# Reading all weights in rows next to each other per partition, and transposing 32x32 blocks on VectorE, in a fused decode layer

## The chip, the cores and the metric

The kernel runs on one core of a Trainium2 chip. The metric is the device time of one execution in microseconds (us), as a median over runs; nearly all executions of one kernel agree within 0.3%.

A profile is one execution on the chip with its records. Its span (138.0 us before) is about 2 us shorter than the timed run. Engines: PE (matmul), PEld (weight load, overlaps PE), DVE (VectorE), ACT (ScalarE), POOL (GpSimd); SPq is the queue of SyncE, from which the loads are issued.

## The reference, cut to what matters

```
h  = x  + attention(layernorm(x)) @ wo        x: 4 x 1 x 1024
h2 = h  + (silu(n @ w1) * (n @ w3)) @ w2      n = layernorm(h)

attention: 32 query heads, 4 KV heads of 128, batch 4, the last 2048 positions of the cache
wq 1024x4096   wo 4096x1024   w1, w3 1024x3584   w2 3584x1024   K, V 4x4x2048x128 each, all bf16
```

There are four rows of activations and 55.6 MB of weights and cache, each byte of which is used once.

## The kernel before

One pool of ten 16 KiB slots per partition takes all loads. They stand in one plan (wq, K, V, wo, w1, w3, w2) and are issued from one queue, ten at the start and then one whenever a slot has been used.

```python
wq_v = A_wq.rearrange("(p kc) n -> p kc n", kc=KC)            # 2 adjacent rows a load: 16 KiB runs
wo_v = A_wo.rearrange("(h4 p r) n -> p h4 r n", p=P, r=RPO)   # 4 adjacent rows:  8 KiB runs
w2_v = B_w2.rearrange("(j p i) n -> p j i n", p=P, i=IF)      # 7 adjacent rows: 14 KiB runs
# w1, w3: rows c*256 ... c*256+255 as "(p r) f -> p r f", r=2:  14 KiB runs, one contiguous block
# K: "g (pp j) d -> pp g (j d)": 16 KiB runs     V: "g (p j) d -> p g j d": 4 KiB runs
...
plan = (
    [("wq", load_wq, (c,)) for c in range(KC // KPC)]
    + [("k", load_k, (b,)) for b in range(B)]
    + [("v", load_v, (b,)) for b in range(B)]
    + [("wo", load_wo, (c,)) for c in range(Hq // HPC)]
    + [("w1", load_w13, (0, c)) for c in range(KC // KPC)]
    + [("w3", load_w13, (1, c)) for c in range(KC // KPC)]
    + [("w2", load_w2, (j, [IF] if j < JG - 1 else [4, 2, 1])) for j in range(JG)]
)
```

Which rows of a weight lie on which partition decides how the activation that is multiplied with it must lie. Before, that costs four selection matmuls and four copies for o, two PE transposes and a copy for the second layernorm, and seven PE transposes and a copy for the gate:

```python
for r in range(RPO):
    nc.tensor.matmul(o4_ps[:, r, :, :, :], lhsT=sel[:, r, :, :], rhs=OT_sb[:], start=True, stop=True)
for hh in range(RPO):
    nc.vector.tensor_copy(out=o4[hh * MP : (hh + 1) * MP, ...], in_=o4_ps[hh * MP : (hh + 1) * MP, :, :, hh, :])
...
for i in range(IF):
    nc.tensor.transpose(out=hg_ps[:, i, :], in_=hg_v[:, i, :], identity=ident[:])
nc.vector.tensor_copy(out=hgT[:, :, :, :, 0], in_=hg_ps[:]...)
```

Of the kernel before, what the change touches and what calls it, by code (L numbers as in the profile page):

```python
# [10 lines left out]
P = 128  # L11
# [8 lines left out]
def kernel(  # L20
# [47 lines left out]
    QD = P // JG  # L68
    CQ = Hq * Dh // JG
# [3 lines left out]
    IF = CF // P  # L73
    PK = P // Hkv
    JK = W // PK
    assert CQ == REP * Dh and CF == IF * P and HF <= 512


    KPC = 2
    HPC = 8  # L80
    RPO = 4
    assert CG == KPC * P
    wq_v = A_wq.rearrange("(p kc) n -> p kc n", kc=KC)
    wo_v = A_wo.rearrange("(h4 p r) n -> p h4 r n", p=P, r=RPO)
    w2_v = B_w2.rearrange("(j p i) n -> p j i n", p=P, i=IF)

    def load_wq(c):
        wq_t = stream.tile([P, KPC, Hq * Dh], BF16, tag="s")
        nc.sync.dma_start(out=wq_t[:], in_=wq_v[:, c * KPC : (c + 1) * KPC, :])
        return wq_t  # L90

    def load_k(b):

        k_t = stream.tile([P, JK * Dh], BF16, tag="s")
        nc.sync.dma_start(
            out=k_t[:],
            in_=A_k_cache[b, :, Sk - W : Sk, :].rearrange("g (pp j) d -> pp g (j d)", pp=PK),
        )
        return k_t

    def load_v(b):
        v_t = stream.tile([P, Hkv, NK, Dh], BF16, tag="s")
        nc.sync.dma_start(
            out=v_t[:],
            in_=A_v_cache[b, :, Sk - W : Sk, :].rearrange("g (p j) d -> p g j d", j=NK),
        )
        return v_t

    def load_wo(c):
        wo_t = stream.tile([P, HPC // RPO, RPO, D], BF16, tag="s")  # L110
        nc.sync.dma_start(
            out=wo_t[:], in_=wo_v[:, c * (HPC // RPO) : (c + 1) * (HPC // RPO), :, :]
        )
        return wo_t

    def load_w13(i, c):
        w13_t = stream.tile([P, KPC, F], BF16, tag="s")
        nc.sync.dma_start(
            out=w13_t[:],
            in_=(B_w1, B_w3)[i][c * KPC * P : (c + 1) * KPC * P, :].rearrange(  # L120
                "(p r) f -> p r f", r=KPC
            ),
        )
        return w13_t

    def load_w2(j, pieces):
        w2_t = stream.tile([P, IF, D], BF16, tag="s")
        i = 0
        for n in pieces:
            nc.sync.dma_start(out=w2_t[:, i : i + n, :], in_=w2_v[:, j, i : i + n, :])  # L130
            i += n
        return w2_t

    plan = (
        [("wq", load_wq, (c,)) for c in range(KC // KPC)]
        + [("k", load_k, (b,)) for b in range(B)]
        + [("v", load_v, (b,)) for b in range(B)]
        + [("wo", load_wo, (c,)) for c in range(Hq // HPC)]
        + [("w1", load_w13, (0, c)) for c in range(KC // KPC)]
        + [("w3", load_w13, (1, c)) for c in range(KC // KPC)]  # L140
        + [("w2", load_w2, (j, [IF] if j < JG - 1 else [4, 2, 1])) for j in range(JG)]
# [4 lines left out]
    def load_next(n=1):  # L146
        for _ in range(n):
            if cursor[0] < len(plan):
                kind, f, args = plan[cursor[0]]
                loaded.setdefault(kind, []).append(f(*args))  # L150
                cursor[0] += 1
# [12 lines left out]
    for j in range(JG):  # L164
        nc.scalar.dma_start(
            out=x_q[QD * j : QD * j + B, :], in_=x_flat[:, j * CG : (j + 1) * CG]
        )
# [20 lines left out]
    for kc in range(KC):  # L188
# [9 lines left out]
    nc.vector.memset(qz[:], 0.0)  # L198

    RS = QD // B  # L200
    spread = const.tile([P, JG, B, RS], FP32)
    nc.vector.memset(spread[:], 0.0)
    nc.vector.tensor_copy(
        out=spread[:, :, :, 0], in_=ident[:].rearrange("p (j x) -> p j x", j=JG)[:, :, :B]
    )
    hgT = act.tile([P, IF, JG, B, RS], BF16)
    nc.gpsimd.memset(hgT[:], 0.0)

    sel = const.tile([P, RPO, RPO, P // RPO], BF16)
    ident_r = ident[:].rearrange("p (m r) -> p r m", r=RPO)  # L210
    for hh in range(RPO):
        nc.vector.tensor_copy(out=sel[:, :, hh, :], in_=ident_r)
# [12 lines left out]
    for kc in range(KC):  # L225
        wq_t = loaded["wq"][kc // KPC]
        for hf in range(CQ // 512):
            for g in range(JG):
                c0 = g * CQ + hf * 512
                nc.tensor.matmul(  # L230
                    q_ps[QD * g : QD * g + B, hf * 512 : (hf + 1) * 512],
                    lhsT=xnT[:, kc, :],
                    rhs=wq_t[:, kc % KPC, c0 : c0 + 512],
                    start=(kc == 0),
                    stop=(kc == KC - 1),
                )
        if kc % KPC == KPC - 1:
            load_next()
# [33 lines left out]
    for u, (b, n) in enumerate(units):  # L272
        k_v = loaded["k"][b][:].rearrange("p (j d) -> p j d", d=Dh)
# [15 lines left out]
        if n == NSB - 1:  # L289
            load_next()  # L290
# [35 lines left out]
    for b in range(B):  # L326
# [10 lines left out]
        load_next()  # L337
    OT_sb = act.tile([P, Hq, B], BF16)
    nc.vector.tensor_copy(out=OT_sb[:].rearrange("p h b -> p b h"), in_=OT_ps[:])

    o4_ps = psA.tile([P, RPO, Hq // RPO, RPO, B], FP32, tag="kt3")
    for r in range(RPO):
        nc.tensor.matmul(o4_ps[:, r, :, :, :], lhsT=sel[:, r, :, :], rhs=OT_sb[:], start=True, stop=True)
    o4 = act.tile([P, Hq // RPO, RPO, B], BF16)
    MP = P // RPO
    for hh in range(RPO):
        nc.vector.tensor_copy(
            out=o4[hh * MP : (hh + 1) * MP, :, :, :].rearrange("p h r b -> p r h b"),
            in_=o4_ps[hh * MP : (hh + 1) * MP, :, :, hh, :],
        )  # L350
# [5 lines left out]
    nc.vector.memset(y_ps[:], 0.0)  # L356
    y2_ps = psB.tile([P, CG], FP32, tag="y2")
    g_ps = psB.tile([P, 2, 512], FP32, tag="g")
    nc.vector.memset(g_ps[:], 0.0)
    u_ps = psB.tile([P, 2, 512], FP32, tag="u")  # L360
    nc.vector.memset(u_ps[:], 0.0)
    for h4 in range(Hq // RPO):
        wo_t = loaded["wo"][h4 * RPO // HPC]
        for r in range(RPO):
            for j in range(JG):
                nc.tensor.matmul(  # L366
                    y_ps[QD * j : QD * j + B, :],
                    lhsT=o4[:, h4, r, :],
                    rhs=wo_t[:, h4 % (HPC // RPO), r, j * CG : (j + 1) * CG],
                    start=(h4 == 0 and r == 0),  # L370
                    stop=(h4 == Hq // RPO - 1 and r == RPO - 1),
                )
        if h4 % (HPC // RPO) == HPC // RPO - 1:
            load_next()
# [40 lines left out]


    def gate_up(kind, out_ps):
        for k2 in range(KC // KPC):
            w_t = loaded[kind][k2]
            for r in range(KPC):  # L420
                for hf in range(2):
                    for j in range(JG):
                        c0 = j * CF + hf * HF
                        nc.tensor.matmul(  # L424
                            out_ps[QD * j : QD * j + B, hf, :HF],
                            lhsT=hnT[:, k2, r, :],
                            rhs=w_t[:, r, c0 : c0 + HF],
                            start=(k2 == 0 and r == 0),
                            stop=(k2 == KC // KPC - 1 and r == KPC - 1),
                        )  # L430
            load_next()
# [67 lines left out]
```

## Time and profile before

| | before |
|---|---|
| time, median of 3 runs | 139.99 us (139.92 to 140.0) |
| span of the profile | 138.0 us |
| HBM read | 55.59 MB, 403 GB/s over the span |
| PE / DVE / ACT busy | 53% / 27% / 21% of the span |

First the page of the kernel before: the span in 40 slices, with the busy tenths of the 16 DMA engines and what they moved; then the packets, the load queue with its packets, MB and share of the engines' time, and the shares of the span in the chain that ended last.

```profile
DMA  5999999999999999999999999999999999999940
GB/s 159 447 410 432 437 423 432 446 418 423 446 401 415 414 420 424 415 431 424 427 432 420 427 434 432 424 436 428 433 424 432 432 420 440 420 445 414 415 197 2
DMA packets 6437, 55.74 MB, mean 404 GB/s; under 512 B 504, under 2 KB 536, under 8 KB 2844
...
q1 hardware_dynamic: 6388, 55.58, 95.4%
...
DMA 61%; PE 22%; ACT 10%; DVE 2%; issue 2%; ACTq 0%
```

DMA is 61% of the chain, and the load engines are busy at nine tenths or more in every slice between the first and the last two. In a fused kernel with five stages that is remarkable: no stage is without loads. So the time is a start (about 2 us until bytes flow: the first slice of 3.45 us has 159 GB/s, which is 1.3 us at full rate), 55.6 MB at some rate, and a tail. A change can win only by a higher rate, fewer bytes, or a shorter start or tail.

The rate can be read off the timeline of the kernel before. Columns: start, duration, engine, line, operation, result and inputs, shapes, count, and in brackets the idle time before it and what ended that. The lines chosen are matmuls that a landing released.

```profile
8.08 1.88 PE L230 MATMUL q_ps<-wq_t,xnT 128*4 128x512 bf16 x16 [2.19 <-DMA wq_t<-in_A_wq_dram]
12.97 1.88 PE L230 MATMUL q_ps<-wq_t,xnT 128*4 128x512 bf16 x16 [3.02 <-DMA wq_t<-in_A_wq_dram]
17.84 1.88 PE L230 MATMUL q_ps<-wq_t,xnT 128*4 128x512 bf16 x16 [3.00 <-DMA wq_t<-in_A_wq_dram]
22.70 1.88 PE L230 MATMUL q_ps<-wq_t,xnT 128*4 128x512 bf16 x16 [2.99 <-DMA wq_t<-in_A_wq_dram]
...
95.86 1.67 PE L424 MATMUL g_ps<-w_t,hnT 128*4 128x448 bf16 x16 [2.57 <-DMA w_t<-in_B_w_dram]
100.10 1.66 PE L424 MATMUL g_ps<-w_t,hnT 128*4 128x448 bf16 x16 [2.57 <-DMA w_t<-in_B_w_dram]
104.36 1.66 PE L424 MATMUL u_ps<-w_t,hnT 128*4 128x448 bf16 x16 [2.60 <-DMA w_t<-in_B_w_dram]
...
125.66 1.69 PE L457 MATMUL y_ps<-w_t,hgT 128*32 128x256 bf16 x28 [2.27 <-DMA w_t<-in_B_w_dram]
129.93 1.69 PE L457 MATMUL y_ps<-w_t,hgT 128*32 128x256 bf16 x28 [2.58 <-DMA w_t<-in_B_w_dram]
```

A wq tile (2.097 MB) comes every 4.87 us, 430.6 GB/s; a w1 or w3 tile (1.835 MB) about every 4.26 us, 430.8 GB/s; a w2 tile every 4.27 us. Ahead of each tile the PE has been idle for over 2 us. wq is the useful control: it already lay as the change lays all weights, 16 KiB at a time, 64 KiB from one partition to the next.

V and wo have no such rhythm, because the attention is behind the stream when they land. For them the windows view shows the bytes: stretch and length, busy time of PE, PEld, DVE, ACT and POOL, granted clock, DMA share, GB/s. V streams in the first two stretches, wo in the third, but for about 1.5 us at the start of the first (still K) and of the third (still V). The view books a packet whole where it starts, so a rate of one window is coarse: one 16 KiB packet more on each of the 16 engines is 0.26 MB, which is 15 GB/s of a window of 17 us.

```profile
40.00:50.00 10.00, 8.89 (x115) 5.74 (x112) 4.15 (x6) 5.75 (x6) 0.00 (x0) 1.00 1.00 410
50.00:58.00 8.00, 6.85 (x84) 4.27 (x83) 2.80 (x5) 4.17 (x5) 0.00 (x0) 1.00 1.02 417
60.00:77.00 17.00, 7.75 (x227) 7.59 (x228) 2.21 (x6) 8.52 (x6) 0.00 (x0) 0.52 1.02 427
```

V (4 KiB runs) is the slowest, 410 to 417 GB/s; wo (8 KiB) has 427.

The last lines of before are those of the o path (78.4 to 81.2 us), of the first two w1 tiles and of the gate (118.9 to 121.7 us), from its timeline:

```profile
78.39 0.44 DVE L339 CAST OT_sb<-OT_ps 128x128 bf16<-128x128 f32 x1 [8.98 <-PE OT_ps L330]
78.89 0.58 PE L343 MATMUL o_ps<-OT_sb,sel 128*128 128x128 bf16 x4 [0.53 <-DVE OT_sb L339]
79.51 1.19 DVE L347 CAST o<-o_ps 32x128 bf16<-32x128 f32 x4 [0.68 <-PE o_ps L343]
80.89 0.27 DVE L356 MEMSET y_ps<- 128x256 f32 x1 [0.20 <-DVE o L347]
81.22 5.30 PE L366 MATMUL y_ps<-wo_t,o 128*4 128x256 bf16 x128 [1.75 <-DVE y_ps L356]
...
90.67 2.62 PE L424 MATMUL g_ps<-w_t,hnT 128*4 128x448 bf16 x32 [0.27 <-DVE hnT L407]
...
120.00 0.96 PE L447 MATMUL hg_ps<-ident,hg 128*128 128x128 bf16 x7 [1.20 <-DVE hg L442]
120.99 0.65 DVE L448 COPY hgT<-hg_ps 128x112 bf16<-128x112 bf16 x1 [1.05 <-PE hg_ps L447]
121.70 1.69 PE L457 MATMUL y_ps<-w_t,hgT 128*32 128x256 bf16 x28 [0.74 <-DVE hgT L448]
```

The wo matmuls start 2.83 us after the attention's result begins to be copied; of the gate's path 1.70 us are transposes, copy and their latencies.

### The profile page before, as it was taken

The numbers are of one execution on the slowest core, as the hardware profiler recorded it, in microseconds if no ns is written. First come the engines' busy times: TensorE is split into PE (matmuls) and PEld (weight loads), VectorE is DVE, ScalarE is ACT, GpSimd is POOL, SyncE is SP. The second block draws the span as 40 slices with busy tenths as digits, with TensorE's granted clock in tenths as the row PEclk, the third lists the DMA queues.
The fourth block names the chain that finished last, engine by engine and source line by source line (L and its number), as shares of the span: only waits on it lengthen the run. The fifth ranks groups of instructions, "written<-read, shape, count | busy, mean of one in ns | idle before, by whom it ended". The sixth has DMA issues, their size and how long they took to land.

```text
span 138.0 us, 2358 instructions
## 1 busy us (share of the span) xinstructions
PE 73.8 (53%) x1057; PEld 44.6 (32%) x1057; DVE 37.7 (27%) x72; ACT 29.1 (21%) x28; POOL 1.5 (1%) x7
## 2 busy tenths in 40 slices
PE   0152354499898989600596649382244422654370
PEld 0110011296565656300586637120011110233330
DVE  6710000242342525450410171510008930310001
ACT  2200000125373737449450000000041000000000
POOL 4000000000000000000000000000000000000000
PEclk9999999999999999975555557975555555555555
DMA  5999999999999999999999999999999999999940
GB/s 159 447 410 432 437 423 432 446 418 423 446 401 415 414 420 424 415 431 424 427 432 420 427 434 432 424 436 428 433 424 432 432 420 440 420 445 414 415 197 2
DMA packets 6437, 55.74 MB, mean 404 GB/s; under 512 B 504, under 2 KB 536, under 8 KB 2844
## 3 DMA queue, kind: packets, MB, share of 16 engines
q1 hardware_dynamic: 6388, 55.58, 95.4%
q8 instruction: 8, 0.13, 0.3%
q10 hardware_dynamic: 40, 0.02, 0.1%
q14 instruction: 1, 0.01, 0.0%
HBM read 55.59 MB, written 0.01 MB: 403 GB/s over the span
## 4 chain that ended last, share of the span: by engine, by line
DMA 61%; PE 22%; ACT 10%; DVE 2%; issue 2%; ACTq 0%
DMA w_t<-in_B_w_dram 41%; DMA k_t<-in_A_k_cache_dram 14%; PE kt_ps L278 11%; DMA wq_t<-in_A_wq_dram 5%; ACT kT L284 5%; PE scores_ps L263 5%; PE OT_ps L330 4%; ACT Pm L302 3%; DVE rmax L297 2%; PE pt_ps L316 1%; ACT L302 1%; PE y_ps L457 1%; ACT PT_sb L322 0%; DVE res L467 0%; DVE Dm L309 0%
## 5 line engine op out<-in xcount | busy, mean ns | idle before, releaser
L278 PE MATMUL kt_ps<-ident,k_t 128*128 128x128 bf16 x256 | 18.8, 237 | 1.0 <-DMA k_t<-in_A_k_cache_dram 1.0
L284 ACT COPY kT<-kt_ps 128x1024 bf16<-128x1024 bf16 x16 | 15.9, 1013 | 15.4 <-PE kt_ps L278 15.4
L278 PEld LDWEIGHTS <-k_t 128*128 128x128 bf16 x256 | 16.6, 107 | 6.1 <-issue 4.9
L282 DVE COPY kT<-kt_ps 128x1024 bf16<-128x1024 bf16 x16 | 11.1, 692 | 18.5 <-PE kt_ps L278 18.5
L230 PE MATMUL q_ps<-wq_t,xnT 128*4 128x512 bf16 x64 | 7.5, 621 | 11.2 <-DMA wq_t<-in_A_wq_dram 11.2
L424 PE MATMUL u_ps<-w_t,hnT 128*4 128x448 bf16 x64 | 6.7, 567 | 10.4 <-DMA w_t<-in_B_w_dram 10.4
L424 PEld LDWEIGHTS <-hnT 128*4 128x4 bf16 x128 | 3.8, 104 | 23.9 <-issue 23.2
L263 PE MATMUL scores_ps<-kT,qz 128*32 128x512 bf16 x64 | 9.9, 610 | 3.0 <-ACT kT L284 3.0
L457 PE MATMUL y_ps<-w_t,hgT 128*32 128x256 bf16 x112 | 7.1, 414 | 6.6 <-DMA w_t<-in_B_w_dram 5.8
L424 PE MATMUL g_ps<-w_t,hnT 128*4 128x448 bf16 x64 | 5.9, 516 | 5.4 <-DMA w_t<-in_B_w_dram 5.1
L330 PE MATMUL OT_ps<-PT_sb,v_t 128*128 128x8 bf16 x256 | 7.4, 168 | 2.0 <-issue 1.8
L330 PEld LDWEIGHTS <-v_t 128*128 128x128 bf16 x256 | 7.3, 104 | 2.2 <-issue 2.1
L457 PEld LDWEIGHTS <-hgT 128*32 128x32 bf16 x112 | 4.5, 135 | 9.2 <-issue 7.3
L230 PEld LDWEIGHTS <-xnT 128*4 128x4 bf16 x64 | 2.0, 106 | 15.9 <-issue 15.5
L316 PE MATMUL pt_ps<-Dm,Pm 128*128 128x128 bf16 x16 | 1.9, 311 | 9.3 <-DVE Dm L309 9.3
L366 PE MATMUL y_ps<-wo_t,o 128*4 128x256 bf16 x128 | 5.3, 344 | 1.7 <-DVE y_ps L356 1.7
L437 DVE RECIPROCAL eg<-eg 128x896 f32<-128x896 f32 x1 | 5.8, 5752 | 0.0
L240 DVE TENSOR_SCALAR q_sb<-q_ps 128x512 bf16<-128x512 f32 x1 | 0.7, 692 | 17.1 <-PE q_ps L230 17.1
L241 ACT ACTIVATE q_sb<-q_ps 128x512 bf16<-128x512 f32 x1 | 0.6, 597 | 20.9 <-DVE q_sb L240 20.9
L316 PEld LDWEIGHTS <-Pm 128*128 128x128 bf16 x16 | 1.6, 146 | 9.8 <-ACT Pm L302 9.8
L302 ACT ACTIVATE Pm<-scores_ps,nmax 128x2048 bf16<-128x2048 f32 x1 | 4.8, 4783 | 0.0
L366 PEld LDWEIGHTS <-o 128*4 128x4 bf16 x128 | 3.5, 105 | 3.5 <-DVE y_ps L356 2.0
(74 smaller groups left out, 40.5 us busy)
## 6 DMA issues: line engine op xcount, KB each, us to landing
w_t<-in_B_w_dram SPq DMA_DIRECT2D x11, 1792.0 KB, 33.3
wq_t<-in_A_wq_dram SPq DMA_DIRECT2D x4, 2048.0 KB, 11.8
k_t<-in_A_k_cache_dram SPq DMA_DIRECT2D x4, 2048.0 KB, 19.5
v_t<-in_A_v_cache_dram SPq DMA_DIRECT2D x4, 2048.0 KB, 38.4
wo_t<-in_A_wo_dram SPq DMA_DIRECT2D x4, 2048.0 KB, 22.9
w_t<-in_B_w_dram SPq DMA_DIRECT2D x1, 1024.0 KB
w_t<-in_B_w_dram SPq DMA_DIRECT2D x1, 512.0 KB, 29.2
w_t<-in_B_w_dram SPq DMA_DIRECT2D x1, 256.0 KB
```

The source lines that it names most:

```text
L230: nc.tensor.matmul(q_ps[QD * g : QD * g + B, hf * 512 : (hf + 1) * 512], lhsT=xnT[:, kc, :], rhs=wq_t[:, kc % KPC, c0 : c0 + 512], start=( ...
L263: nc.tensor.matmul(scores_ps[QD * g : QD * (g + 1), n * 512 : (n + 1) * 512], lhsT=qz[:, b, g * QD : (g + 1) * QD], rhs=kT_v[:, g, :, :], ...
L278: nc.tensor.transpose(out=kt_ps[:, jj, :], in_=k_v[:, n * NJ + t * TB + jj, :], identity=ident[:])
L282: nc.vector.tensor_copy(out=kT[:, t * TB : (t + 1) * TB, :], in_=kt_ps[:])
L284: nc.scalar.copy(out=kT[:, t * TB : (t + 1) * TB, :], in_=kt_ps[:])
L302: nc.scalar.activation(out=Pm[:].rearrange("q (c jq) -> q jq c", jq=NSB), in_=scores_ps[:].rearrange("q (jq c) -> q jq c", jq=NSB), func=A ...
L316: nc.tensor.matmul(pt_ps[:, jj, :], lhsT=Pm[:, (jb * JPB + jj) * P : (jb * JPB + jj + 1) * P], rhs=Dm[:], start=True, stop=True)
L330: nc.tensor.matmul(OT_ps[:, b, g * REP : (g + 1) * REP], lhsT=v_t[:, g, j, :], rhs=PT_sb[:, j, g * QD + b * REP : g * QD + (b + 1) * REP], ...
L366: nc.tensor.matmul(y_ps[QD * j : QD * j + B, :], lhsT=o4[:, h4, r, :], rhs=wo_t[:, h4 % (HPC // RPO), r, j * CG : (j + 1) * CG], start=(h4 ...
L424: nc.tensor.matmul(out_ps[QD * j : QD * j + B, hf, :HF], lhsT=hnT[:, k2, r, :], rhs=w_t[:, r, c0 : c0 + HF], start=(k2 == 0 and r == 0), s ...
L437: nc.vector.reciprocal(out=eg[:], in_=eg[:])
L457: nc.tensor.matmul(y2_ps[QD * j : QD * (j + 1), :], lhsT=hgT[:, i, jf, :, :].rearrange("p b s -> p (b s)"), rhs=w2_t[:, i, j * CG : (j + 1 ...
```

## The change

The intent: give every partition rows of a weight that are adjacent in HBM, so that a load is one long run per partition, and choose the row order so that the activations come into place by 32x32 block transposes, which VectorE does in one instruction without the PE and PSUM. The core of the diff:

```diff
-    wo_v = A_wo.rearrange("(h4 p r) n -> p h4 r n", p=P, r=RPO)
-    w2_v = B_w2.rearrange("(j p i) n -> p j i n", p=P, i=IF)
+    wo_v = A_wo.rearrange("(p i) n -> p (i n)", i=IO)     # 32 rows a partition, 8 a load: 16 KiB runs
+    w1_v = B_w1.rearrange("(p i) n -> p (i n)", i=KC)     # 8 rows a partition, 2 a load: 14 KiB, 56 KiB apart
+    w3_v = B_w3.rearrange("(p i) n -> p (i n)", i=KC)
+    w2_v = B_w2.rearrange("(p i) n -> p (i n)", i=IF)     # 28 rows: loads of 8, 8, 5, 4, 2, 1
 ...
-    for r in range(RPO):
-        nc.tensor.matmul(o4_ps[:, r, :, :, :], lhsT=sel[:, r, :, :], rhs=OT_sb[:], start=True, stop=True)
-    (four copies)
+    nc.vector.transpose(out=oT[:]..., in_=OT_sb[:]...)
+    nc.tensor.matmul(o4_ps[:], lhsT=perm[:], rhs=oT[:], start=True, stop=True)
+    nc.vector.tensor_copy(out=o4[:, :, :, 0], in_=o4_ps[:].rearrange("p b i -> p i b"))
-    nc.vector.memset(y_ps[:], 0.0)      # and g_ps, u_ps: the matmuls now write all 32 rows of a group
 ...
-    (two PE transposes of hn, one copy)
+    nc.vector.transpose(out=hnT[:]..., in_=hn[:].rearrange("q (c k) -> q k c", k=KC))
 ...
-    (seven PE transposes of hg, one copy)
+    nc.vector.transpose(out=hgT[:]..., in_=hg[:]....rearrange("q (c i) -> q i c", i=IF))
```

K's and V's loads, the plan's order, the ten slots and the last pieces (4, 2 and 1 rows) stay. The matmuls of wo, w1 and w3 load 32 weight columns instead of 4.

More of the change, by code (lines that the diff above doesn't have):

```diff
@@ L68 @@
     QD = P // JG
+    RS = QD // B
     CQ = Hq * Dh // JG
@@ L72 @@
     HF = CF // 2
-    IF = CF // P
+    IO = Hq * Dh // P
+    IF = F // P
     PK = P // Hkv
     JK = W // PK
-    assert CQ == REP * Dh and CF == IF * P and HF <= 512
-    KPC = 2
-    HPC = 8
-    RPO = 4
-    assert CG == KPC * P
-    wq_v = A_wq.rearrange("(p kc) n -> p kc n", kc=KC)
-    wo_v = A_wo.rearrange("(h4 p r) n -> p h4 r n", p=P, r=RPO)
-    w2_v = B_w2.rearrange("(j p i) n -> p j i n", p=P, i=IF)
-    def load_wq(c):
-        wq_t = stream.tile([P, KPC, Hq * Dh], BF16, tag="s")
-        nc.sync.dma_start(out=wq_t[:], in_=wq_v[:, c * KPC : (c + 1) * KPC, :])
-        return wq_t
@@ L92, in load_k @@
-    def load_k(b):
-        k_t = stream.tile([P, JK * Dh], BF16, tag="s")
-        nc.sync.dma_start(
-            out=k_t[:],
-            in_=A_k_cache[b, :, Sk - W : Sk, :].rearrange("g (pp j) d -> pp g (j d)", pp=PK),
-        )
-        return k_t
-    def load_v(b):
-        v_t = stream.tile([P, Hkv, NK, Dh], BF16, tag="s")
-        nc.sync.dma_start(
-            out=v_t[:],
-            in_=A_v_cache[b, :, Sk - W : Sk, :].rearrange("g (p j) d -> p g j d", j=NK),
-        )
-        return v_t
@@ L109, in load_wo @@
-    def load_wo(c):
-        wo_t = stream.tile([P, HPC // RPO, RPO, D], BF16, tag="s")
-        nc.sync.dma_start(
-            out=wo_t[:], in_=wo_v[:, c * (HPC // RPO) : (c + 1) * (HPC // RPO), :, :]
-        )
-        return wo_t
-    def load_w13(i, c):
-        w13_t = stream.tile([P, KPC, F], BF16, tag="s")
-        nc.sync.dma_start(
-            out=w13_t[:],
-            in_=(B_w1, B_w3)[i][c * KPC * P : (c + 1) * KPC * P, :].rearrange(
-                "(p r) f -> p r f", r=KPC
-            ),
-        )
-        return w13_t
@@ L126, in load_w2 @@
-    def load_w2(j, pieces):
-        w2_t = stream.tile([P, IF, D], BF16, tag="s")
-        i = 0
-        for n in pieces:
-            nc.sync.dma_start(out=w2_t[:, i : i + n, :], in_=w2_v[:, j, i : i + n, :])
-            i += n
-        return w2_t
-    plan = (
-        [("wq", load_wq, (c,)) for c in range(KC // KPC)]
-        + [("k", load_k, (b,)) for b in range(B)]
-        + [("v", load_v, (b,)) for b in range(B)]
-        + [("wo", load_wo, (c,)) for c in range(Hq // HPC)]
-        + [("w1", load_w13, (0, c)) for c in range(KC // KPC)]
-        + [("w3", load_w13, (1, c)) for c in range(KC // KPC)]
-        + [("w2", load_w2, (j, [IF] if j < JG - 1 else [4, 2, 1])) for j in range(JG)]
+    assert CQ == REP * Dh and HF <= 512 and CG == QD * KC and CF == QD * IF and IO == QD == Hq
@@ new lines, with load_rows @@
+    SLOT = 8192
+    RQ = 2
+    RO = 8
+    BS = 1
+    wq_v = A_wq.rearrange("(p i) n -> p (i n)", i=KC)
+    wo_v = A_wo.rearrange("(p i) n -> p (i n)", i=IO)
+    w1_v = B_w1.rearrange("(p i) n -> p (i n)", i=KC)
+    w3_v = B_w3.rearrange("(p i) n -> p (i n)", i=KC)
+    w2_v = B_w2.rearrange("(p i) n -> p (i n)", i=IF)
+    def load_rows(src, n, r0, pieces):
+        t = stream.tile([P, SLOT], BF16, tag="s")
+        i = 0
+        for m in pieces:
+            nc.sync.dma_start(
+                out=t[:, i * n : (i + m) * n], in_=src[:, (r0 + i) * n : (r0 + i + m) * n]
+            )
+            i += m
+        return [t[:, k * n : (k + 1) * n] for k in range(i)]
@@ new lines, in load_k @@
+    def load_k(b):
+        t = stream.tile([P, SLOT], BF16, tag="s")
+        out = []
+        for k in range(BS):
+            v = t[:, k * JK * Dh : (k + 1) * JK * Dh]
+            nc.sync.dma_start(
+                out=v,
+                in_=A_k_cache[b + k, :, Sk - W : Sk, :].rearrange("g (pp j) d -> pp g (j d)", pp=PK),
+            )
+            out.append(v)
+        return out
+    def load_v(b):
+        t = stream.tile([P, SLOT], BF16, tag="s")
+        out = []
+        for k in range(BS):
+            v = t[:, k * JK * Dh : (k + 1) * JK * Dh].rearrange("p (g j d) -> p g j d", g=Hkv, d=Dh)
+            nc.sync.dma_start(
+                out=v,
+                in_=A_v_cache[b + k, :, Sk - W : Sk, :].rearrange("g (p j) d -> p g j d", j=NK),
+            )
+            out.append(v)
+        return out
@@ new lines @@
+    N_Q, N_F = Hq * Dh, F
+    plan = (
+        [("wq", load_rows, (wq_v, N_Q, c, [RQ])) for c in range(0, KC, RQ)]
+        + [("k", load_k, (b,)) for b in range(0, B, BS)]
+        + [("v", load_v, (b,)) for b in range(0, B, BS)]
+        + [("wo", load_rows, (wo_v, D, c, [RO])) for c in range(0, IO, RO)]
+        + [("w1", load_rows, (w1_v, N_F, c, [RQ])) for c in range(0, KC, RQ)]
+        + [("w3", load_rows, (w3_v, N_F, c, [RQ])) for c in range(0, KC, RQ)]
+        + [("w2", load_rows, (w2_v, D, 0, [8])), ("w2", load_rows, (w2_v, D, 8, [8])),
+           ("w2", load_rows, (w2_v, D, 16, [5])), ("w2", load_rows, (w2_v, D, 21, [4, 2, 1]))]
@@ L149, in load_next @@
                 kind, f, args = plan[cursor[0]]
-                loaded.setdefault(kind, []).append(f(*args))
+                loaded.setdefault(kind, []).extend(f(*args))
                 cursor[0] += 1
@@ L165 @@
         nc.scalar.dma_start(
-            out=x_q[QD * j : QD * j + B, :], in_=x_flat[:, j * CG : (j + 1) * CG]
+            out=x_q[QD * j : QD * (j + 1) : RS, :], in_=x_flat[:, j * CG : (j + 1) * CG]
         )
@@ L198 @@
     nc.vector.memset(qz[:], 0.0)
-    RS = QD // B
-    spread = const.tile([P, JG, B, RS], FP32)
-    nc.vector.memset(spread[:], 0.0)
+    ident_f = const.tile([P, P], FP32)
+    nc.vector.tensor_copy(out=ident_f[:], in_=ident[:])
+    perm = const.tile([P, P], BF16)
     nc.vector.tensor_copy(
-        out=spread[:, :, :, 0], in_=ident[:].rearrange("p (j x) -> p j x", j=JG)[:, :, :B]
-    )
-    hgT = act.tile([P, IF, JG, B, RS], BF16)
-    nc.gpsimd.memset(hgT[:], 0.0)
-    sel = const.tile([P, RPO, RPO, P // RPO], BF16)
-    ident_r = ident[:].rearrange("p (m r) -> p r m", r=RPO)
-    for hh in range(RPO):
-        nc.vector.tensor_copy(out=sel[:, :, hh, :], in_=ident_r)
+        out=perm[:].rearrange("p (h dq) -> p h dq", dq=JG),
+        in_=ident[:].rearrange("p (dq h) -> p h dq", dq=JG),
+    )
+    o4 = act.tile([P, IO, B, RS], BF16)
+    nc.gpsimd.memset(o4[:], 0.0)
     same = const.tile([P, JG, QD], FP32)
@@ L225 @@
     for kc in range(KC):
-        wq_t = loaded["wq"][kc // KPC]
+        wq_t = loaded["wq"][kc]
         for hf in range(CQ // 512):
@@ L232 @@
                     lhsT=xnT[:, kc, :],
-                    rhs=wq_t[:, kc % KPC, c0 : c0 + 512],
+                    rhs=wq_t[:, c0 : c0 + 512],
                     start=(kc == 0),
@@ L236 @@
                 )
-        if kc % KPC == KPC - 1:
+        if kc % RQ == RQ - 1:
             load_next()
@@ L272 @@
     for u, (b, n) in enumerate(units):
-        k_v = loaded["k"][b][:].rearrange("p (j d) -> p j d", d=Dh)
+        k_v = loaded["k"][b].rearrange("p (j d) -> p j d", d=Dh)
         kT = ktpool.tile([P, NJ, P], BF16, tag="kT")
@@ L288 @@
             emit_scores(u - 1)
-        if n == NSB - 1:
+        if n == NSB - 1 and b % BS == BS - 1:
             load_next()
@@ L336 @@
                 )
-        load_next()
-    OT_sb = act.tile([P, Hq, B], BF16)
-    nc.vector.tensor_copy(out=OT_sb[:].rearrange("p h b -> p b h"), in_=OT_ps[:])
-    o4_ps = psA.tile([P, RPO, Hq // RPO, RPO, B], FP32, tag="kt3")
-    for r in range(RPO):
-        nc.tensor.matmul(o4_ps[:, r, :, :, :], lhsT=sel[:, r, :, :], rhs=OT_sb[:], start=True, stop=True)
-    o4 = act.tile([P, Hq // RPO, RPO, B], BF16)
-    MP = P // RPO
-    for hh in range(RPO):
-        nc.vector.tensor_copy(
-            out=o4[hh * MP : (hh + 1) * MP, :, :, :].rearrange("p h r b -> p r h b"),
-            in_=o4_ps[hh * MP : (hh + 1) * MP, :, :, hh, :],
-        )
+        if b % BS == BS - 1:
+            load_next()
+    OT_sb = act.tile([P, B, Hq], BF16)
+    nc.vector.tensor_copy(out=OT_sb[:], in_=OT_ps[:])
+    oT = act.tile([P, B, IO], BF16)
+    nc.vector.transpose(out=oT[:].rearrange("p b i -> p (b i)"), in_=OT_sb[:].rearrange("p b h -> p (b h)"))
+    o4_ps = psA.tile([P, B, IO], FP32, tag="kt3")
+    nc.tensor.matmul(o4_ps[:], lhsT=perm[:], rhs=oT[:], start=True, stop=True)
+    nc.vector.tensor_copy(out=o4[:, :, :, 0], in_=o4_ps[:].rearrange("p b i -> p i b"))
     psA_cm.__exit__(None, None, None)
@@ L355 @@
     y_ps = psB.tile([P, CG], FP32, tag="y")
-    nc.vector.memset(y_ps[:], 0.0)
     y2_ps = psB.tile([P, CG], FP32, tag="y2")
     g_ps = psB.tile([P, 2, 512], FP32, tag="g")
-    nc.vector.memset(g_ps[:], 0.0)
     u_ps = psB.tile([P, 2, 512], FP32, tag="u")
-    nc.vector.memset(u_ps[:], 0.0)
-    for h4 in range(Hq // RPO):
-        wo_t = loaded["wo"][h4 * RPO // HPC]
-        for r in range(RPO):
-            for j in range(JG):
-                nc.tensor.matmul(
-                    y_ps[QD * j : QD * j + B, :],
-                    lhsT=o4[:, h4, r, :],
-                    rhs=wo_t[:, h4 % (HPC // RPO), r, j * CG : (j + 1) * CG],
-                    start=(h4 == 0 and r == 0),
-                    stop=(h4 == Hq // RPO - 1 and r == RPO - 1),
-                )
-        if h4 % (HPC // RPO) == HPC // RPO - 1:
+    for i in range(IO):
+        for j in range(JG):
+            nc.tensor.matmul(
+                y_ps[QD * j : QD * (j + 1), :],
+                lhsT=o4[:, i, :, :].rearrange("p b s -> p (b s)"),
+                rhs=loaded["wo"][i][:, j * CG : (j + 1) * CG],
+                start=(i == 0),
+                stop=(i == IO - 1),
+            )
+        if i % RO == RO - 1:
             load_next()
@@ L400 @@
     )
-    hn_ps = psB.tile([P, KPC, P], BF16, tag="tp")
-    hn_v = hn[:].rearrange("q (p r) -> q r p", r=KPC)
-    for r in range(KPC):
-        nc.tensor.transpose(out=hn_ps[:, r, :], in_=hn_v[:, r, :], identity=ident[:])
-    hnT = act.tile([P, JG, KPC, B], BF16)
-    nc.vector.tensor_copy(
-        out=hnT[:], in_=hn_ps[:].rearrange("p r (j x) -> p j r x", j=JG)[:, :, :, :B]
-    )
-    nc.tensor.matmul(
-        y2_ps[:], lhsT=spread[:].rearrange("p j b s -> p (j b s)"), rhs=h1[:],
-        start=True, stop=False, skip_group_check=True,
-    )
+    hnT = act.tile([P, KC, QD], BF16)
+    nc.vector.transpose(
+        out=hnT[:].rearrange("p k x -> p (k x)"), in_=hn[:].rearrange("q (c k) -> q k c", k=KC)
+    )
+    nc.tensor.matmul(y2_ps[:], lhsT=ident_f[:], rhs=h1[:], start=True, stop=False, skip_group_check=True)
     def gate_up(kind, out_ps):
-        for k2 in range(KC // KPC):
-            w_t = loaded[kind][k2]
-            for r in range(KPC):
-                for hf in range(2):
-                    for j in range(JG):
-                        c0 = j * CF + hf * HF
-                        nc.tensor.matmul(
-                            out_ps[QD * j : QD * j + B, hf, :HF],
-                            lhsT=hnT[:, k2, r, :],
-                            rhs=w_t[:, r, c0 : c0 + HF],
-                            start=(k2 == 0 and r == 0),
-                            stop=(k2 == KC // KPC - 1 and r == KPC - 1),
-                        )
-            load_next()
+        for k in range(KC):
+            for hf in range(2):
+                for j in range(JG):
+                    c0 = j * CF + hf * HF
+                    nc.tensor.matmul(
+                        out_ps[QD * j : QD * (j + 1), hf, :HF],
+                        lhsT=hnT[:, k, :],
+                        rhs=loaded[kind][k][:, c0 : c0 + HF],
+                        start=(k == 0),
+                        stop=(k == KC - 1),
+                    )
+            if k % RQ == RQ - 1:
+                load_next()
     gate_up("w1", g_ps)
@@ L442 @@
     nc.vector.tensor_tensor(out=hg[:], in0=u_ps[:, :, :HF], in1=gs[:], op=ALU.mult)
-    hg_ps = psB.tile([P, IF, P], BF16, tag="tp")
-    hg_v = hg[:].rearrange("q s c -> q (s c)").rearrange("q (p i) -> q i p", i=IF)
-    for i in range(IF):
-        nc.tensor.transpose(out=hg_ps[:, i, :], in_=hg_v[:, i, :], identity=ident[:])
-    nc.vector.tensor_copy(
-        out=hgT[:, :, :, :, 0], in_=hg_ps[:].rearrange("p i (j x) -> p i j x", j=JG)[:, :, :, :B]
-    )
-    for jf in range(JG):
-        w2_t = loaded["w2"][jf]
-        for i in range(IF):
-            for j in range(JG):
-                nc.tensor.matmul(
-                    y2_ps[QD * j : QD * (j + 1), :],
-                    lhsT=hgT[:, i, jf, :, :].rearrange("p b s -> p (b s)"),
-                    rhs=w2_t[:, i, j * CG : (j + 1) * CG],
-                    start=False,
-                    stop=(jf == JG - 1 and i == IF - 1),
-                    skip_group_check=True,
-                )
+    hgT = act.tile([P, IF, QD], BF16)
+    nc.vector.transpose(
+        out=hgT[:].rearrange("p i x -> p (i x)"),
+        in_=hg[:].rearrange("q s c -> q (s c)").rearrange("q (c i) -> q i c", i=IF),
+    )
+    for i in range(IF):
+        for j in range(JG):
+            nc.tensor.matmul(
+                y2_ps[QD * j : QD * (j + 1), :],
+                lhsT=hgT[:, i, :],
+                rhs=loaded["w2"][i][:, j * CG : (j + 1) * CG],
+                start=False,
+                stop=(i == IF - 1),
+                skip_group_check=True,
+            )
     res = act.tile([P, CG], BF16)
```

## The prediction

> **What bounds the kernel now.** The load stream, throughout. The page's DMA row is at 9 tenths in all slices but three; the load queue is busy 95.4% of the span and moves 55.6 MB. In the chain of waits DMA is 61%; its PE and ACT pieces (27 to 77 us) only release buffers for loads that queue anyway (w tiles land 25 to 34 us after issue). Matmuls of wq, w1, w3 and w2 start on a landing; PE then idles until the next.
>
> **Rate by layout, from the timeline (starts of matmuls that a landing releases).** wq (already p-major, 16 KiB runs, partitions 64 KiB apart): 8.08, 12.97, 17.84, 22.70, so 4.87 us for 2.097 MB = 430.6 GB/s. w1/w3 (14 KiB runs, contiguous block): every 4.26 us for 1.835 MB = 430.8. w2 (14 KiB runs): 4.27 us, 430. wo (8 KiB runs), from the windows view: 425 to 429. Only V (4 KiB runs, unchanged) is lower, 415 to 422. The Trainium skill (DMA: Bandwidth & Descriptors, "Where 436 GB/s comes from") gives a ceiling of 435 GB/s for 16 engines; the trace agrees: no tile interval is faster than 431.
>
> **What the change does.**
> - wo, 8 to 16 KiB runs: 427 to 430.7 GB/s over 8.39 MB, an estimate of 0.1 to 0.2 us gained.
> - w2, 14 to 16 KiB runs: wq and w1 have the same rate at these sizes, so 0.
> - w1/w3: same runs, now 56 KiB apart instead of contiguous: wq is the control, 64 KiB apart at full rate, so 0. The same page ("Latency and other measured facts") warns of slow row pitches from 512 KiB up; none here is as large.
> - o: four selection matmuls, four 0.29 us copies and a 0.27 us memset (78.9 to 81.2 us) become a block transpose, a matmul, a copy: about 1 us less before the wo matmuls. LN2: two transposes and a copy (90.1 to 90.6) become one block transpose, about equal. Gate: 120.0 to 121.7 us (7 transposes 0.96, copy 0.65) becomes one 128x896 block transpose, estimated 1.1 us from the 128x896 multiply that takes 1.09 (2 if its strided read is slow).
> - wo's, w1's and w3's matmuls get 32 weight columns instead of 4; the streamed columns set the time (w2 already runs so: 28 in 1.69 us), so equal but for the clock.
>
> **How much is critical.** None of the compute edits: after LN2 the PE has caught up and idles 2.6 us before each tile; after the gate it has used the first w2 tile 2.3 us before the second lands. The tail is untouched: last landing 133.6, last matmul 134.7, copy, output DMA, end 138.0; the last pieces remain 4, 2, 1 rows. Only wo's 0.1 to 0.2 us remains.
>
> **Prediction.** 139.8 us, 139.1 to 140.7 eight times in ten. Chances: faster by over 2% 0.02, within 2% 0.94, slower by over 2% 0.04.
>
> **What would show it.** Intervals of w1 and w3 tiles still 4.26 us and of 16 KiB tiles 4.87; wo's window at 430 GB/s; some 512 fewer packets; wo matmuls about 1 us earlier, w1 matmuls from the third tile on unmoved; last landing within 0.5 us of 133.6.
>
> **What would make it wrong.** The 56 KiB pitch of w1/w3/w2 falling on fewer memory channels than a contiguous block (5% on 22 MB is 2.6 us); engines drifting apart; a block transpose many times slower than estimated (it would need over 5 us to matter).

## The result, and the profile after

| | before | after |
|---|---|---|
| time, median of 6 runs | 139.88 us (139.79 to 140.0) | 139.81 us (139.62 to 140.12) |
| ratio, 95% interval | | 0.9995 (0.9982 to 1.0008) |
| span of the profile | 138.0 us | 137.7 us |
| DMA packets | 6437 | 5925 |

A ratio is the mean time of one kernel's fast runs over that of the other's of the same rounds, so it is not quite the ratio of the medians.

The page of the kernel after, the same lines:

```profile
DMA  5999999999999999999999999999999999999950
GB/s 155 419 425 438 423 433 438 423 433 428 428 429 395 420 420 420 416 439 448 433 419 438 428 419 423 433 416 446 421 433 421 437 429 444 428 419 430 410 226 2
DMA packets 5925, 55.74 MB, mean 405 GB/s; under 512 B 504, under 2 KB 536, under 8 KB 2844
...
q1 hardware_dynamic: 5876, 55.58, 95.6%
...
DMA 63%; PE 21%; ACT 10%; DVE 2%; issue 1%; ACTq 0%; SPq 0%
```

There are 512 packets fewer, as many as wo's longer runs save, and the stream is as full as before. The windows of V and of wo in the kernel after:

```profile
40.00:50.00 10.00, 8.61 (x108) 5.36 (x104) 3.63 (x6) 5.89 (x6) 0.00 (x0) 1.00 1.00 410
50.00:58.00 8.00, 6.40 (x84) 4.17 (x80) 3.53 (x5) 3.95 (x4) 0.00 (x0) 1.00 1.03 420
60.00:77.00 17.00, 8.29 (x247) 8.13 (x248) 1.80 (x4) 8.32 (x6) 0.00 (x0) 0.50 1.02 435
```

wo's window went from 427 to 435 GB/s, which is within one packet for each engine, and V's is what it was. The timeline of the kernel after: the o path, then three w1 tiles, then the gate and two w2 tiles.

```profile
77.85 0.29 DVE L333 CAST OT_sb<-OT_ps 128x128 bf16<-128x128 f32 x1 [9.17 <-PE OT_ps L323]
78.17 0.31 DVE L336 STREAM_TRANSPOSE oT<-OT_sb 128x128 bf16<-128x128 bf16 x1
78.54 0.29 PE L338 MATMUL o_ps<-oT,perm 128*128 128x128 bf16 x1 [0.73 <-DVE oT L336]
78.87 0.72 DVE L339 CAST o<-o_ps 128x128 bf16<-128x128 f32 x1 [0.38 <-PE o_ps L338]
79.65 5.09 PE L350 MATMUL y_ps<-t,o 128*32 128x256 bf16 x128 [0.82 <-DVE o L339]
...
91.31 1.68 PE L399 MATMUL g_ps<-t,hnT 128*32 128x448 bf16 x16 [0.88 <-DMA t<-in_B_w_dram]
95.55 1.68 PE L399 MATMUL g_ps<-t,hnT 128*32 128x448 bf16 x16 [2.55 <-DMA t<-in_B_w_dram]
99.81 1.69 PE L399 MATMUL g_ps<-t,hnT 128*32 128x448 bf16 x16 [2.58 <-DMA t<-in_B_w_dram]
...
119.75 1.70 DVE L421 STREAM_TRANSPOSE hgT<-hg 128x896 bf16<-128x896 bf16 x1
121.73 1.90 PE L429 MATMUL y_ps<-t,hgT 128*32 128x256 bf16 x32 [3.16 <-DMA t<-in_B_w_dram]
126.58 1.90 PE L429 MATMUL y_ps<-t,hgT 128*32 128x256 bf16 x32 [2.95 <-DMA t<-in_B_w_dram]
```

The o path takes 1.80 us instead of 2.83 (79.65 minus 77.85). What came of that microsecond stands in the next lines: before, the PE went through the first two w1 tiles without a wait between them (32 matmuls from 90.67 us); now it waits 0.88 us for the second, until it lands, and ahead of the third it waits as long as before (2.55 us against 2.57). The gate's block transpose takes 1.70 us, the same 1.70 us as the seven transposes, the copy and their latencies before; and its result then waits for the w2 tile anyway, which is now 8 rows instead of 7. Tiles come every 4.26 us (w1) and 4.85 us (w2, 2.097 MB, 432 GB/s).

### The profile page after: what moved, and what is told of

The parts are those of the page before. It is cut to its first block, busy times and chain, and to the rows that moved or that the text cites. A ratio compares the mean times of both kernels' runs of the same rounds, so it can differ in the third digit from the quotient of the medians.

```text
span 137.7 us, 2324 instructions
## 1 busy us (share of the span) xinstructions
PE 71.8 (52%) x1045; PEld 44.5 (32%) x1045; DVE 36.4 (26%) x63; ACT 29.1 (21%) x28; POOL 1.6 (1%) x7
## 2 busy tenths in 40 slices
DMA packets 5925, 55.74 MB, mean 405 GB/s; under 512 B 504, under 2 KB 536, under 8 KB 2844
## 4 chain that ended last, share of the span: by engine, by line
DMA 63%; PE 21%; ACT 10%; DVE 2%; issue 1%; ACTq 0%; SPq 0%
DMA t<-in_B_w_dram 43%; DMA t<-in_A_k_cache_dram 14%; PE kt_ps L271 11%; DMA t<-in_A_wq_dram 5%; ACT kT L277 5%; PE scores_ps L256 5%; ACT Pm L295 3%; PE OT_ps L323 2%; DVE rmax L290 2%; PE y_ps L429 2%; PE pt_ps L309 1%; ACT L295 1%; ACT PT_sb L315 0%; DVE res L439 0%; DVE Dm L302 0%
## 5 line engine op out<-in xcount | busy, mean ns | idle before, releaser
L271 PE MATMUL kt_ps<-ident,t 128*128 128x128 bf16 x256 | 18.1, 232 | 1.0 <-DMA t<-in_A_k_cache_dram 1.0
L271 PEld LDWEIGHTS <-t 128*128 128x128 bf16 x256 | 15.9, 104 | 6.1 <-issue 4.9
L399 PEld LDWEIGHTS <-hnT 128*32 128x32 bf16 x128 | 4.9, 128 | 26.2 <-issue 23.6
L223 PE MATMUL q_ps<-t,xnT 128*4 128x512 bf16 x64 | 7.5, 621 | 10.2 <-DMA t<-in_A_wq_dram 10.2
L399 PE MATMUL u_ps<-t,hnT 128*32 128x448 bf16 x64 | 6.7, 573 | 10.3 <-DMA t<-in_B_w_dram 10.3
L429 PE MATMUL y_ps<-t,hgT 128*32 128x256 bf16 x112 | 7.1, 413 | 8.7 <-DMA t<-in_B_w_dram 8.6
L399 PE MATMUL g_ps<-t,hnT 128*32 128x448 bf16 x64 | 6.4, 550 | 8.3 <-DMA t<-in_B_w_dram 6.0
L323 PE MATMUL OT_ps<-PT_sb,t 128*128 128x8 bf16 x256 | 7.4, 168 | 2.2 <-issue 2.0
L323 PEld LDWEIGHTS <-t 128*128 128x128 bf16 x256 | 7.3, 104 | 2.4 <-issue 2.3
L350 PE MATMUL y_ps<-t,o 128*32 128x256 bf16 x128 | 5.1, 335 | 0.8 <-DVE o L339 0.8
L295 ACT ACTIVATE Pm<-scores_ps,nmax 128x2048 bf16<-128x2048 f32 x1 | 4.8, 4784 | 0.0
L412 DVE TENSOR_SCALAR eg<-eg 128x896 f32<-128x896 f32 x1 | 0.6, 627 | 14.8 <-ACT eg L411 14.8
```

Of the source, the lines that this page charges most:

```text
L223: nc.tensor.matmul(q_ps[QD * g : QD * g + B, hf * 512 : (hf + 1) * 512], lhsT=xnT[:, kc, :], rhs=wq_t[:, c0 : c0 + 512], start=(kc == 0), ...
L271: nc.tensor.transpose(out=kt_ps[:, jj, :], in_=k_v[:, n * NJ + t * TB + jj, :], identity=ident[:])
L295: nc.scalar.activation(out=Pm[:].rearrange("q (c jq) -> q jq c", jq=NSB), in_=scores_ps[:].rearrange("q (jq c) -> q jq c", jq=NSB), func=A ...
L323: nc.tensor.matmul(OT_ps[:, b, g * REP : (g + 1) * REP], lhsT=v_t[:, g, j, :], rhs=PT_sb[:, j, g * QD + b * REP : g * QD + (b + 1) * REP], ...
L350: nc.tensor.matmul(y_ps[QD * j : QD * (j + 1), :], lhsT=o4[:, i, :, :].rearrange("p b s -> p (b s)"), rhs=loaded["wo"][i][:, j * CG : (j + ...
L399: nc.tensor.matmul(out_ps[QD * j : QD * (j + 1), hf, :HF], lhsT=hnT[:, k, :], rhs=loaded[kind][k][:, c0 : c0 + HF], start=(k == 0), stop=( ...
```

## The experiments

The theory: the stream is the only limit. Compute edits are worth nothing as long as they stay inside the waits for tiles; the layout is worth what it does to the rate; and the rate depends on the length of the runs only weakly. The rival: the change contains a gain and a loss of similar size that cancel, for example a shorter compute path against a slower layout of w1 and w3.

All kernels below are the kernel after with one edit (in experiment 6, several that belong together). Each was timed side by side with the kernel before, so a difference from the kernel after is one between two sets of rounds; the kernel before had medians of 139.88 to 139.93 us in them. Those that load other rows than the arithmetic expects give a wrong result. Even so the comparison with the reference passed them: x dominates the output, and a pass here says little about the attention or the MLP. It missed this too: as printed, every kernel here, the one before included, feeds the score matmuls with `lhsT=qz[:, b, g * QD : (g + 1) * QD]`, which adds the scores of all four batches into the same eight rows of each KV head. The slice that gives each batch its own rows is `qz_v[:, z0 : z0 + QD]`, whose two names stand in the kernel unused (with it, a replay of the printed attention in double precision agrees with the reference; as printed it does not); do not copy these kernels without it. The slices have the same shape in all kernels, so the comparisons of times stand.

### 1. The new compute with all loads in the old layout

```diff
-    wo_v = A_wo.rearrange("(p i) n -> p (i n)", i=IO)
+    wo_v = A_wo.rearrange("(h4 p r) n -> p h4 (r n)", p=P, r=4)
-    w1_v = B_w1.rearrange("(p i) n -> p (i n)", i=KC)      # w3 likewise
+    w1_v = B_w1.rearrange("(c p r) n -> p c (r n)", p=P, r=RQ)
-    w2_v = B_w2.rearrange("(p i) n -> p (i n)", i=IF)
+    w2_v = B_w2.rearrange("(j p i) n -> p j (i n)", p=P, i=7)
```

> The new kernel's compute (block transposes, 32-column weights) with every load in the old layout (wo 8 KiB runs, w2 14 KiB, w1/w3 in contiguous blocks); wrong result on purpose. Theory (the load stream is the only limit, the compute edits are worth 0): same as the kernel before, 139.9 us, ratio 0.999 to 1.001, wo window back to 427 GB/s. Rival (the shorter o and LN2 path saves about 1 us and the new layout costs it again): 138.9 us, ratio 0.993.

Measured: 139.98 us, ratio 1.0005 (0.9994 to 1.0017), wo's window back at 427 GB/s:

```profile
60.00:77.00 17.00, 8.90 (x271) 8.74 (x272) 1.80 (x4) 8.15 (x6) 0.00 (x0) 0.50 1.01 427
```

So the compute edits alone are worth nothing, though the wo matmuls of this run start at 79.03 us instead of 81.22. (1.03 us of that is the shorter o path; for the rest, the V matmuls happened to end earlier in this execution.) The rival's gain of 0.7% is excluded. Between this kernel and the kernel after lies the layout alone: 139.98 to 139.81 us, a step that the two intervals do not resolve, since they overlap.

### 2. w1 and w3 back in contiguous blocks

```diff
-        + [("w1", load_rows, (w1_v, N_F, c, [RQ])) for c in range(0, KC, RQ)]      # w3 likewise
+        + [("w1", load_block, (w1_v, N_F, c)) for c in range(KC // RQ)]            # rows c*256 ... c*256+255
```

> The new kernel with only w1 and w3 back in contiguous blocks of 256 rows, same 14 KiB runs; wrong result on purpose. Theory (a 56 KiB distance between partitions costs nothing): 139.8 us, ratio 0.998 to 1.001, tile intervals 4.26 us. Rival (the distance costs what the longer runs of wo gain, so the two cancel): faster than the new kernel by 0.2 to 0.5 us, 139.4 us, ratio 0.996.

Measured: 139.73 us, ratio 0.999 (0.9978 to 1.0002); tiles at 95.50 and 99.75 (w1) and 104.01 us (w3), so every 4.25 us against 4.26 in the kernel after. The distance of 56 KiB between partitions costs less than these runs resolve. The 0.08 us between the two medians lies inside the spread of either kernel's runs, and the ratio is not the 0.996 that the rival needed.

### 3. wo in runs of 2 KiB

The effect of run length in the change is too small to see, so it was enlarged.

```diff
-    wo_v = A_wo.rearrange("(p i) n -> p (i n)", i=IO)
+    wo_v = A_wo.rearrange("(i p) n -> p i n", p=P)         # one row a run; 4096 packets instead of 512
```

> The new kernel with wo read in 2 KiB runs (4096 packets instead of 512) from a contiguous block; wrong result on purpose. Theory (each packet has a cost; V's 4 KiB runs lose about 0.6 us over 2048 packets against 16 KiB runs): 0.6 us / 1536 packets x 3584 packets = 1.4 us more, 141.2 us, ratio 1.009; wo window near 400 GB/s. Rival (run length from 2 KiB up costs nothing, V is slow for another reason): 139.8 us, ratio 0.999.

Measured: 140.91 us, ratio 1.0072 (1.006 to 1.0084). wo's window in the windows view of this kernel:

```profile
60.00:77.00 17.00, 8.81 (x267) 8.65 (x268) 1.80 (x4) 8.04 (x6) 0.00 (x0) 0.50 1.04 406
```

435 became 406 GB/s, and the time rose by 1.10 us over the kernel after, for 3584 packets more: 0.31 ns of the stream per packet (0.30 from the two ratios), or, since 16 engines share them, about 4.9 ns of one engine (16 x 0.31). I had expected 1.4 us from V's window; the direction holds, the size was a quarter too high.

### 4. V in runs of 16 KiB

V's loads were not touched by the change, and they are the ones with short runs.

```diff
-  in_=A_v_cache[b + k, :, Sk - W : Sk, :].rearrange("g (p j) d -> p g j d", j=NK),
+  in_=A_v_cache[b + k, :, Sk - W : Sk, :].rearrange("g (pp j) d -> pp g (j d)", pp=PK),
```

> The new kernel with V read in 16 KiB runs as K is (512 packets instead of 2048); wrong result on purpose. Theory (V's 415 GB/s comes from its 4 KiB runs): V's window at 428 to 431 GB/s and 0.6 us faster, 139.2 us, ratio 0.995. Rival (V's window is slow because of the K transposes that run at the same time): window still at 415, 139.8 us, ratio 0.999.

Measured: 139.34 us, ratio 0.9967 (0.9951 to 0.9984). The two windows in which V streams:

```profile
40.00:50.00 10.00, 8.61 (x109) 5.39 (x108) 3.79 (x6) 5.97 (x6) 0.00 (x0) 1.00 1.00 424
50.00:58.00 8.00, 6.56 (x84) 4.17 (x80) 3.36 (x5) 3.95 (x4) 0.00 (x0) 1.00 1.03 436
```

410 and 420 became 424 and 436 while the K transposes ran beside them as before, so it was the runs and not the neighbours. The gain over the kernel after, for 1536 packets fewer, is 0.47 us by the medians and 0.39 us by the two ratios, 0.31 or 0.25 ns per packet. With 0.31 the change's own 512 packets are worth an estimated 0.16 us; the layout alone (experiment 1 against the kernel after) measured 0.17, but inside the noise.

The kept traces settle this more finely. They hold the start, duration and size of every packet; with each packet's bytes spread evenly over its duration, one can read when a tensor's last byte is through (worked out from the trace files; `prof` has no such view). Time in us from the end of one tensor to the end of the next:

| | before | loads as before (1) | after | w1, w3 in blocks (2) | wo 2 KiB (3) | V 16 KiB (4) |
|---|---|---|---|---|---|---|
| V | 20.12 | 20.07 | 20.07 | 20.07 | 20.08 | 19.63 |
| wo | 19.76 | 19.78 | 19.63 | 19.60 | 20.74 | 19.57 |
| w1 and w3 | 34.28 | 34.31 | 34.32 | 34.34 | 34.32 | 34.37 |

Where a layout did not change, the runs agree within about 0.1 us. wo gained 0.15 us from 8 to 16 KiB (1 against after, 0.29 ns for each of 512 packets) and lost 1.11 us at 2 KiB (0.31 ns); V gained 0.44 us (0.29 ns). So about 0.3 ns per packet fits three changes of the packet count, from 512 to 3584, and w1 and w3 take the same time in both layouts.

### 5. A longer gate path

```diff
+    for _ in range(1 + 3):        # and 1 + 6
         nc.vector.transpose(out=hgT[:]..., in_=hg[:]...)
```

> The new kernel with the gate's block transpose done three more times (3 x 1.70 = 5.1 us more between the last w3 matmul and the first w2 matmul). Theory (the PE has over 6 us of room there: transposed at 126.6 us, 112 matmuls of 60 ns, done at 133.3, before the 134.4 of now): 139.8 us, ratio 0.998 to 1.001. Rival (the gate lies on the critical path): 144.9 us.

> The same with six more block transposes, 10.2 us. Theory (room used up: transposed at 131.7, 112 matmuls of 60 ns, done at 138.4 instead of 134.4): 143.8 us, ratio 1.028. If the room is larger than I count, less.

Measured: 139.76 us, ratio 0.999 (0.9976 to 1.0004), where the trace has 6.90 us of gate transposes instead of 1.70; 142.28 us (141.74 to 142.65), ratio 1.0177 (1.016 to 1.0193), where it has 12.10 us. The first w2 matmuls of the one, and the transposes of the other:

```profile
126.66 4.46 PE L430 MATMUL y_ps<-t,hgT 128*32 128x256 bf16 x84 [8.12 <-DVE hgT L422]
```

```profile
119.73 12.10 DVE L422 STREAM_TRANSPOSE hgT<-hg 128x896 bf16<-128x896 bf16 x7
```
In the first, w2's matmuls start 4.9 us later than in the kernel after (126.66 us instead of 121.73) and all of it disappears. In the second the room is used up, and 2.47 us come out. So a change of this path is free up to an estimated 8 us (12.10 minus 1.70 minus 2.47 is 7.9; 7.6 to 8.5 over the spread of these runs), and whether the block transposes are faster or slower than the PE's by some tenths cannot matter.

I had expected 4 us, from 60 ns per w2 matmul. The windows view of the last stage, first the kernel after and then the kernel with six more transposes, shows the difference (the granted clock is the third number from the end):

```profile
131.00:138.00 7.00, 2.07 (x28) 1.03 (x27) 0.42 (x1) 0.00 (x0) 0.00 (x0) 0.50 0.27 107
```

```profile
131.00:138.00 7.00, 4.45 (x112) 3.41 (x112) 1.25 (x2) 0.00 (x0) 0.00 (x0) 0.76 0.25 98
```

The mean granted clock is 0.76 instead of 0.50, and 112 matmuls took 4.45 us, 40 ns each. Work that has piled up is done faster here than the same work in small portions after each landing. Which rule grants the clock these runs do not show.

### 6. A real kernel with V in runs of 16 KiB

Experiment 4 gives a wrong result: with 16 KiB runs a V tile holds 32 partitions of each KV head, interleaved, and the probabilities must lie on the same partitions, with zeros for the other three heads. Here that is done with constant 0/1 matrices: sixteen matmuls of 512 columns spread the transposed probabilities, and sixteen more copies take them out of PSUM into one of the ten slots. The algebra was checked against plain attention in double precision, where it agrees to rounding error once the score matmuls take the slice named above.

```diff
+    vsel = const.tile([P, 4, Hkv, P], BF16)      # vsel[(jj pp), jj', g, (pp' g')] = 1 if jj=jj', pp=pp', g=g'
+    PT_t = stream.tile([P, SLOT], BF16, tag="s") # in place of the load after the last K tile
-        out=Pm[:].rearrange("q (c jq) -> q jq c", jq=NSB), in_=scores_ps[:].rearrange(...),
+        out=Pm[:], in_=scores_ps[:],
 ...
+    for jj in range(4):
+        for g in range(Hkv):
+            px_ps = psA.tile([P, NK, QD], FP32, tag=f"kt{nx % 4}")
+            nc.tensor.matmul(px_ps[:], lhsT=vsel[:, jj, g, :], rhs=T_sb[:, :, g * QD : (g + 1) * QD], ...)
+            (copy to PT_v[:, jj, :, g * QD : (g + 1) * QD], DVE and ACT in turn)
 ...
-    (256 V matmuls of 8 columns)
+    (256 V matmuls of 32 columns, rhs = PT_sb[:, j, the columns of b])
```

> The new kernel with V really read in 16 KiB runs (right result by its algebra): the transposed probabilities are spread over partitions by 16 selection matmuls of 512 columns and 16 more evictions, an estimate of 5 to 7 us more before the V matmuls. Theory (1536 packets fewer at 0.31 ns of the stream each, and the added compute fits in the waits for w1 and w3): 139.3 us, ratio 0.9955 to 0.998, wo matmuls starting at 84 to 87 us instead of 79.7. Rival (the attention stage has no such room): over 140.5 us.

Measured: 139.23 us, ratio 0.9949 (0.9934 to 0.9963) over its four fast runs. A fifth, the profiled one, was slow (141.71 us, granted clock 0.64), and so was one run of the kernel before in this set (185.57 us); neither is in the ratio. In the slow profile the stream fell to 359 GB/s between 83 and 87 us. There the first load that needs a V slot was issued at 82.66 us (74.58 in the fast profile below), after V matmuls that started 8 us later; that this let the stream run dry is inferred. The same kernel ran once more:

> The same kernel as v_16k_true again, because its profile fell in the slow state. Theory: in a fast profile the V window has 424 to 436 GB/s as in v_16k, the wo matmuls start at 84 to 87 us, no slice of the load stream falls under 400 GB/s between 10 and 130 us, and the time is 139.2 us, ratio 0.995 again. Rival (the slow profile's gap in the stream at about 84 us is a fault of the kernel, not of the state): the gap stands in the fast profile too.

Measured: 139.32 us, ratio 0.9955 (0.9941 to 0.9968), fast profile. From its timeline:

```profile
61.09 1.97 ACT L305 ACTIVATE Pm<-scores_ps,nmax 128x2048 bf16<-128x2048 f32 x1
66.31 5.89 PE L332 MATMUL px_ps<-T_sb,vsel 128*128 128x512 bf16 x16 [0.67 <-ACT T_sb L325]
83.61 5.14 PE L372 MATMUL y_ps<-t,o 128*32 128x256 bf16 x128 [0.81 <-DVE o L361]
99.25 0.94 PE L421 MATMUL g_ps<-t,hnT 128*32 128x448 bf16 x16 [2.06 <-DMA t<-in_B_w_dram]
```

The wo matmuls start 4.0 us later than in the kernel after, at 83.61 us, and by the last w1 tile the PE is again waiting for the stream (2.06 us). No slice between 10 and 130 us falls under 400 GB/s; that the kernel has less room left stands. This is the one version with the algebra in order (but for the score slice that all share) that beat both kernels outside the intervals, by about 0.5%, with more compute than either.

## Why the prediction was right

- **The stream is the limit.** Right. The o path became 1.03 us shorter (2.83 to 1.80) and the gate path was lengthened by 5.2 us, and neither moved the time.
- **Rates by layout.** Right for w1, w3 and w2: intervals of 4.26 and 4.85 us, and contiguous blocks gave the same (experiment 2). wq had been a good control. The fear named at the end of the prediction, that a pitch of 56 KiB costs 5%, did not come true. The Trainium skill (DMA: Bandwidth & Descriptors, "Latency and other measured facts") lists slow pitches of 512 KiB and more, measured on copies between HBM tensors; that nothing is lost at 56 and 64 KiB does not contradict it. The prediction's "none here is as large" holds of the weights and not of K (last section).
- **wo's gain of 0.1 to 0.2 us.** Right in size by the packet records: 0.15 us. The times alone do not show it: 0.17 us for the layout alone lies inside the noise, and against the kernel before, in its own rounds, 0.07 us were measured, in an interval that holds zero. The windows view shows more (427 to 435 GB/s in one window of 17 us would be 0.3 us); it is not fine enough for this.
- **The ceiling.** The skill's page puts the fabric's at 435 GB/s ("Where 436 GB/s comes from"). The tiles came at 430 to 433 GB/s (a single w1 interval was 4.24 us, so "no tile interval is faster than 431" was slightly off), which agrees. Slices and windows above 435, up to 448, can come from booking whole packets. The same passage has loads from HBM bound at about 358 GB/s; here, with one core running, they were not (430.6 for wq). That no layout could have brought much fits the ceiling, but what set the rate was not tested.
- **Sizes that were off.** The strided 128x896 block transpose took 1.70 us, not the 1.1 us estimated from a multiply of the same shape (the prediction allowed for 2). wo's matmuls started 1.57 us earlier and not 1 (79.65 against 81.22), of which the o path is 1.03. w1's matmuls from the third tile on were said to stay in place; they moved 0.3 us earlier (95.86 to 95.55), with the landing that releases them. The last load packet ended at 133.60 us (133.87 before), within the forecast. "It would need over 5 us to matter" was on the safe side: the room is about 8 us.
- **Not settled.** Whether w2 gained: its stretch, measured like those above, is 18.18 and 18.04 us in the two profiles with its old layout and 17.91 to 18.00 in those with the new, but it ends with the slowest engine's last packet, and two profiles are few. The tenth of a microsecond between the medians of the kernel after and of the one with contiguous w1 and w3 is not in their stretches (34.32 and 34.34 us). The effect of runs longer than 16 KiB was not tried.

## What to carry to other kernels

When the loads fill the whole span, first read the rate of each tensor's stretch, and look for the slowest: here it was V, which the change left alone, and not the weights that it rearranged. Run length costs by the packet (about 0.3 ns of the stream each here), so 8 to 16 KiB on 8 MB is worth a tenth of a per cent, and 4 to 16 KiB three times that. Compute beside such a stream is not worth shortening, but it can be lengthened as far as the waits reach: the version that gained spent more PE, DVE and ACT time to allow a better load.

## What the Trainium skill lacked or had wrong

- DMA: Bandwidth & Descriptors ("Why small descriptors are slow") gives a fixed cost of about 3 cycles per packet, and speaks of it as a matter of 256-byte descriptors. The runs show a cost of about 4.6 to 4.9 ns of an engine per packet that is still measurable from 4 to 16 KiB (V: 0.44 us in 139.8). Whether it is the same cost no run here shows.
- The same page has no table of rate against run length for long runs in a full stream. These runs give, by the packet records over a whole tensor: 2 KiB 404 GB/s (wo), 4 KiB 417 to 418 (V), 8 KiB 424 (wo), 14 KiB 427 to 428 (w1 and w3), 16 KiB 427 to 429 (wo, V, K).
- Its row on power-of-two pitches begins at 512 KiB and has no smaller ones. Here 64 KiB (wq) and 56 KiB (w1, w3 of the kernel after) ran at 430.6 and 430.8 GB/s. K, whose neighbouring partitions are 2 MiB apart in groups of four, had 428 to 431 GB/s in the kernel before (27.4 to 37.2 us), where the page has a large loss at a pitch of 2 MiB; it is not the same pattern.
- VectorE: DVE Perf Modes ("The three transpose paths") has 311 ns for 128x128 on VectorE, and the trace has exactly that (311 ns, read without a stride). No page has a time for a block transpose with a strided input: 128x256 took 626 ns and 128x896 took 1697 ns, both strided, so 1.67 ns per further column (1071 ns over 640 columns), where Vector Engine (DVE) Microarchitecture Reference ("The reshape front-end and per-opcode configuration") says one element per cycle per lane. That the stride is the cause was not tested.
- No page has a time for a strided write by ScalarE: the exponential of 128x2048 took 4784 ns when it wrote bf16 with a stride of four elements, and 1967 ns when it wrote them in order (the kernel after against the last kernel above). It cost nothing here: the attention was made longer in experiment 6 and the time did not rise.
